# A table that gives every step of the prologue and of the first four chunks its own place, with the low half of the hidden layer issued one slot later

## The chip, the cores and the metric

One core of a Trainium2 chip runs the whole kernel. The time is device microseconds of one execution. Before the change three runs gave 982.63 us as the median (981.52 to 983.33).

## The reference

```python
def _attn_ref(q, k, v):                  # q, k, v: (8, 8, 576, 64)
    ...
    mask_plain = (rel >= 0) & (rel < window)                                     # heads 0-3, window 32
    mask_dil = (rel >= 0) & (rel < window * dilation) & (rel % dilation == 0)    # heads 4-7, dilation 4
    ...
    scores = np.where(masks[None, :, :, :], scores, -1000000000.0)
    scores = scores - np.max(scores, axis=-1, keepdims=True)
    attn = np.exp(scores)
    attn = attn / (np.sum(attn, axis=-1, keepdims=True) + 1e-09)
    return np.matmul(attn, v)

def _moe_ref(x, U, V, w_ch1, w_ch2):     # x: (8, 576, 512), U: (576, 32), V: (32, 576)
    xt = x.transpose(0, 2, 1)
    h = xt @ U @ V
    u = x + h.transpose(0, 2, 1)
    ch = np.maximum(u @ w_ch1, 0.0) @ w_ch2     # 512 -> 2048 -> 512
    return u + ch
```

A banded attention over 8 batches gives x; a mixing of rank 32 along the tokens is added to x; a two-layer network with 2048 hidden units and a ReLU follows, added to its own input. U, V, w_ch1 and w_ch2 come as 64-bit floats and are narrowed on the chip.

## The kernel before

**Tiling.** The 4608 tokens are 36 tiles of 128. The network works through them in 12 chunks: chunk 0 has four tiles, chunk 1 two, the others three. For each of 16 slices f of the hidden layer a chunk computes ph (12 matmuls, line 872) from the input and the first layer's weights, each split into a high and a low part; ACT makes hh = relu(ph) rounded (line 877), DVE makes the rest, hl = relu(ph) - hh (line 878), and the products of slice f-1 with the second layer go into acc, three matmuls per tile (line 891: hh with the high weight, hh with the low weight, hl with the high weight). So hl of slice f is wanted only after the ph of slice f+1 and the first two matmuls of acc f.

**Attention** goes in groups g of two blocks of 64 queries, nine groups to a batch (g = 0 to 71). A group's steps are: scores (PE, line 302), add (DVE, 313), top (DVE, 321), exp (ACT, 331 in the prologue, 333 later), the transposition of the weights (on PE and a copy by ACT, 339 and 345/348, for g below 18; on DVE, 355, after that), the products with v (PE, 373), and the weighting of the result (`weighted`: DVE 386, 387, 413), which also frees the PSUM bank. `burst(g, p)` puts the products of group p and the scores of group g on PE; `after_burst` is the weighting of p and the add of g.

**Mixing** of a batch b: `split_x` (ACT 446, POOL 447; 463 and 465 in the prologue) splits x into two parts, `t_mm` (PE 494; 484 and 480 in the prologue) multiplies by U, `t_evict` (501, 502) brings it to SBUF, `mix` (PE 511) multiplies by V and `mix_add` (DVE 517) adds it to x. `lay_x`, `lay_mix`, `split_sums` (PE 526 and 532, ACT 542, DVE 544) build the input of chunk 0. `turn_x` and `take_x` (DVE 563, DMA 567 and 574) transpose later tiles through DRAM.

**Weights.** The 32 pieces (j odd: the first layer's, j even: the second layer's, from j = 1 on) are fetched, then put through five stages: `w_first` (ACT 176, 177), two merges on DVE (181, 185), the high part (ACT 242), the low part (line 245: POOL, or DVE where j % 3 == 2). They are made in the course of chunk 0.

**Order.** Each engine works its queue in order, and the order is the program's. The prologue is a loop over s = 0 to 10, with lists that say what is added after which step. From chunk 0 on the network's loop calls `slot()` twice within ph, once after hl, and once after each tile of acc (7 slots to a slice in chunk 0, 5 in chunk 1, 6 later). A sorted list holds everything else with the slot at which it is issued:

```python
    def slot():
        n_slot[0] += 1
        while queue and queue[0][0] <= n_slot[0]:
            queue.pop(0)[2]()
```

`step_at(g)` is the slot of the burst of group g, between marks in STEP_AT, and every other step of g stands a number of slots behind it.

Of the kernel before, what the change touches and what calls it, by code (L numbers as in the profile page):

```python
# [123 lines left out]
def attention_moe_kernel(ctx: ExitStack, tc: tile.TileContext, qk, vv, masks, ident, ut, vt, w1, w2, out):  # L124
# [253 lines left out]
    def weighted(g):  # L378
# [26 lines left out]
        for dst, row, both in parts:  # L405
            rs = slice(row, P if both == 2 else row + QB)
            for u, pv in enumerate(pvs):
                o = dst[rs, u * P:(u + 1) * P].rearrange("p (h d) -> p h d", d=D)
# [4 lines left out]
                nc.vector.tensor_tensor(out=o, in0=pv[rs, :, 0:D],  # L413
                                        in1=ssum[rs, u].unsqueeze(2).broadcast_to([rs.stop - rs.start, 2, D]), op=ALU.mult)
# [262 lines left out]

    def both(fn, *args):
        return lambda: fn(*args)

    todo = {"act": [(2, v_steps[0]), (3, u_steps[0]), (4, both(split_v, 0)), (5, both(split_u, 0)), (6, both(keep_v, 0)), (7, both(keep_v, 1))],
            "dve": [(3, v_steps[1]), (3, v_steps[2]), (4, u_steps[1]), (4, u_steps[2])],
            "pool": [(5, both(split_v, 1)), (6, both(split_u, 1))]}
    for s, i, c in ((4, 1, 1), (5, 2, 1), (6, 3, 1), (7, 4, 1), (7, 0, 1), (8, 4, 0), (8, 0, 0), (9, 1, 0), (10, 2, 0)):
        todo["act"].append((s, both(split_first, i, c)))
        todo["pool"].append((s + (s < 10), lambda i=i, c=c: rest[i, c]()))
# [47 lines left out]
    t_first(1, 0)
    t_first(2, 0)
    t_first(3, 0)
    lay_x(2, 0)
    lay_x(CT, 0)
    for t in range(2):
        split_sums(t, 1, 1)  # L740
    t_evict(0, 0)
    for t in range(CT + 1):
        lay_mix(t, 0)
        split_sums(t, 0, 0)
    for t in range(2, CT + 1):
        split_sums(t, 1, 1)
    for t in range(CT + 1):
        split_sums(t, 0, 1)
        sums.pop(t)
    for s in range(NGB + LAG, NGB + LAG + 4):  # L750
        run_todo("act", s)
        run_todo("dve", s)
# [33 lines left out]
    LAST = [step_at(2 * NGB - 1) + 9.6, step_at(2 * NGB - 1) + 13.1]  # L786
    for i, at_ in enumerate(LAST):
        g = 2 * NGB - LAG + i
        add(step_at(2 * NGB - 1) + 1 + i, take_v, g)
        add(at_, burst, -1, g)  # L790
        add(at_ + 1, after_burst, -1, g)
    for g in range(NGB, NG + LAG):
        at_ = step_at(g)
# [23 lines left out]
    for b in range(1, B):
        for c in (1, 0):
            if c == 1:
                first = step_at(NGB * b + ODD + LAG) + (9 if b == 1 else 12)  # L820
# [157 lines left out]
```

## Time and profile before

| | |
|---|---|
| median of three runs | 982.63 us (981.52 to 983.33) |
| the profiled execution | 982.7 us, span 980.8 us |
| PE, DVE, ACT, POOL busy | 942.0, 600.0, 281.1, 109.3 us |
| instructions on PE / DVE / ACT / POOL | 9000 / 1953 / 735 / 139 |
| DMA | 94.30 MB, 96 GB/s over the span |

The span leaves 1.9 us of the profiled execution outside. A busy time of PE does not say that PE ran at its best pace: matmuls are pipelined, and one that has started late or runs slowly counts as busy. Idle time of PE with the name of what ended it, stage by stage, and the pitch from one matmul to the next are read instead.

### The profile page before, as it was taken

The page shows a single profiled execution, that of the slowest core. Times are in us where ns is not written, and L with a number is a line of the kernel's source. Part 1 is how long each engine was busy: PE and PEld are TensorE (multiplying, and loading weights), DVE is VectorE, ACT ScalarE, POOL GpSimd, SP SyncE. Part 2 cuts the span into 40 slices and gives each one's busy share as a digit, 9 for nine tenths or more (in the row PEclk, how much of TensorE's full clock was granted, in tenths as well). Part 3 has the DMA queues.
Part 4 walks back from the last instruction along what each step waited for, and adds up shares of the span by engine and source line. Part 5 has one row for each costly group of instructions (what it writes and reads, how often), then busy time and mean ns, then how long its engine had stood idle before and what let it go on. Part 6 is the DMA issues. An engine that isn't in the chain of part 4 may idle for free.

```text
span 980.8 us, 22338 instructions
## 1 busy us (share of the span) xinstructions
PE 942.0 (96%) x9000; PEld 815.3 (83%) x9000; DVE 600.0 (61%) x1953; ACT 281.1 (29%) x735; POOL 109.3 (11%) x139
## 2 busy tenths in 40 slices
PE   6999989989999999999999999999999999999998
PEld 4777668878878788888888888888888889999997
DVE  5677776877768777666766766756766753211211
ACT  4687662222212232122222222122211311111110
POOL 4332251001100110010100110010100100000000
PEclk9999999999999999999999999999999999999999
DMA  9577632243243224132233322322224201101000
GB/s 328 153 222 237 215 107 90 85 137 92 64 134 99 60 75 127 61 112 69 87 86 93 102 70 77 113 83 80 81 61 120 82 23 34 54 22 43 33 1 33
DMA packets 79144, 94.30 MB, mean 96 GB/s; under 512 B 8256, under 2 KB 57536, under 8 KB 79040
## 3 DMA queue, kind: packets, MB, share of 16 engines
q1 hardware_dynamic: 79040, 92.86, 30.5%
q8 instruction: 71, 1.16, 0.5%
q14 instruction: 33, 0.27, 0.1%
HBM read 70.81 MB, written 22.02 MB: 95 GB/s over the span
## 4 chain that ended last, share of the span: by engine, by line
PE 72%; DVE 9%; issue 9%; ACT 5%; POOL 3%; DMA 2%; SPq 1%; POOLq 0%; ACTq 0%; DVEq 0%
PE ph L872 33%; PE acc L891 31%; PE att L302 2%; POOL xhl L447 2%; DVE pt L355 2%; PE att L373 2%; ACT p L333 1%; PE t L494 1%; ACT hh L877 1%; DMA qk<-qk 1%; DVE vw L185 1%; PE m L511 1%; DMA v<-vv 1%; DVE top L321 1%; DVE p L313 1%
## 5 line engine op out<-in xcount | busy, mean ns | idle before, releaser
L878 DVE SCALAR_TENSOR_TENSOR hl<-ph,hh 128x384 fp32r<-128x384 f32 (+2 forms) x192 | 106.9, 557 | 275.4 <-ACT hh L877 274.0
L891 PE MATMUL acc<-w2h,hh 128*128 128x512 f32 x576 | 229.2, 398 | 2.8 <-ACT hh L877 2.8
L891 PE MATMUL acc<-w2h,hl 128*128 128x512 f32 x576 | 228.0, 396 | 2.0 <-DVE hl L878 2.0
L891 PE MATMUL acc<-w2l,hh 128*128 128x512 f32 x576 | 227.6, 395 | 2.3 <-POOL w2l L245 2.3
L355 DVE STREAM_TRANSPOSE pt<-p 32x64 f32<-32x64 f32 x864 | 203.8, 236 | 33.8 <-ACT p L333 20.3
L877 ACT ACTIVATE hh<-ph 128x384 fp32r<-128x384 f32 (+2 forms) x192 | 93.6, 488 | 455.3 <-PE ph L872 451.8
L872 PE MATMUL ph<-uth,w1h 128*128 128x384 f32 (+2 forms) x768 | 168.1, 340 | 0.1
L872 PE MATMUL ph<-uth,w1l 128*128 128x384 f32 (+2 forms) x768 | 167.4, 339 | 0.0
L872 PE MATMUL ph<-utl,w1h 128*128 128x384 f32 (+2 forms) x768 | 166.6, 338 | 0.0
L872 PEld LDWEIGHTS ph<-uth,w1h 128*128 128x128 f32 x768 | 135.6, 189 | 17.0 <-ACT uth L598 0.6
L872 PEld LDWEIGHTS ph<-uth,w1l 128*128 128x128 f32 x768 | 133.7, 188 | 4.0
L872 PEld LDWEIGHTS ph<-utl,w1h 128*128 128x128 f32 x768 | 132.5, 188 | 3.8
L891 PEld LDWEIGHTS acc<-w2h,hl 128*128 128x128 f32 x576 | 108.4, 188 | 27.6 <-DVE hl L878 3.7
L891 PEld LDWEIGHTS acc<-w2h,hh 128*128 128x128 f32 x576 | 108.6, 189 | 21.6 <-ACT hh L877 3.4
L891 PEld LDWEIGHTS acc<-w2l,hh 128*128 128x128 f32 x576 | 108.5, 188 | 18.7 <-POOL w2l L245 3.1
L447 POOL TENSOR_TENSOR xhl<-x,xhl 128x256 fp32r<-128x256 f32 (+1 forms) x70 | 52.5, 762 | 606.5 <-ACT xhl L446 426.9
L333 ACT ACTIVATE p<-p,top 128x64 f32<-128x64 f32 x252 | 68.9, 337 | 164.4 <-DVE top L321 164.3
L302 PE MATMUL att<-qk 64*32 64x64 f32 x2304 | 43.8, 236 | 9.4 <-DMA qk<-qk 6.2
L302 PEld LDWEIGHTS att<-qk 64*32 64x32 f32 x2304 | 34.7, 111 | 13.5 <-DMA qk<-qk 6.2
L313 DVE SCALAR_TENSOR_TENSOR p<-att,mask_sb 128x128 f32<-128x128 f32 x144 | 34.4, 279 | 13.7 <-PE att L302 13.5
L373 PEld LDWEIGHTS att<-v,pt 64*32 64x32 f32 x2016 | 19.3, 106 | 21.8 <-issue 18.0
L446 ACT CAST xhl<-x 128x256 fp32r<-128x256 f32 (+1 forms) x70 | 26.6, 401 | 27.6 <-DVE x L413 14.8
(94 smaller groups left out, 630.6 us busy)
## 6 DMA issues: line engine op xcount, KB each, us to landing
qk<-qk SPq DMA_DIRECT2D x64, 288.0 KB, 3.9
v<-vv SPq DMA_DIRECT2D x126, 130.0 KB, 3.5
raw<-w SPq DMA_DIRECT2D x25, 512.0 KB, 4.4
out<-x SPq DMA_DIRECT2D x36, 256.0 KB, 2.1
zd<-z SPq DMA_DIRECT2D x120, 64.0 KB, 1.8
xt<-zd SPq DMA_DIRECT2D x30, 256.0 KB, 2.7
xd<-xp SPq DMA_DIRECT2D x32, 128.0 KB, 2.1
x<-xd SPq DMA_DIRECT2D x32, 128.0 KB, 2.6
```

The lines of the kernel that those rows point to most:

```text
L185: nc.vector.scalar_tensor_tensor(out=vi, in0=vi, scalar=3, in1=s32, op0=ALU.logical_shift_left, op1=ALU.bitwise_or)
L302: nc.tensor.matmul(att[h][r * WIN:(r + 1) * WIN, u * KB:(u + 1) * KB], lhsT=q_, rhs=k_, start=True, stop=True, tile_position=(h * D, r * WIN))
L313: nc.vector.scalar_tensor_tensor(out=p_sb[:, h], in0=att[h][:, 0:2 * KB].rearrange("p (u k) -> p u k", k=KB), scalar=1.0 / 8.0, in1=m, op0 ...
L333: nc.scalar.activation(out=p4[:, n], in_=p4[:, n], func=AF.Exp, bias=top[:, n:n + 1])
L355: nc.vector.transpose(out=pts[g % 2][ks, :, rs], in_=p_sb[rs, :, u, WIN * k:WIN * (k + 1)])
L373: nc.tensor.matmul(att[u][row:row + WIN, o:o + DV], lhsT=pt[us_, h, WIN * r:WIN * (r + 1)], rhs=loaded[g, 1][r // 2][us_, r % 2, h * DV:(h ...
L446: nc.scalar.copy(out=xhl[rs, 0], in_=x[rs])
L447: nc.gpsimd.tensor_tensor(out=xhl[rs, 1], in0=x[rs], in1=xhl[rs, 0].bitcast(F32), op=ALU.subtract)
L872: nc.tensor.matmul(ph, lhsT=w[:, k, :], rhs=u[:, k, :], start=(n == 0 and m == 0), stop=(n == 2 and m == KC - 1))
L877: nc.scalar.activation(out=hh, in_=ph, func=AF.Relu)
L878: nc.vector.scalar_tensor_tensor(out=hl, in0=ph, scalar=0.0, in1=hh.bitcast(F32), op0=ALU.max, op1=ALU.subtract)
L891: nc.tensor.matmul(acc[i], lhsT=h[:, ss], rhs=w, start=(c > 1 and f == 1 and n == 0), stop=(f == FC and n == 2))
```

## The change

The prologue's loop is replaced by a list of named steps. Each has a place (a number) and the steps that must stand before it; the places are in the table `AT`, where a name with no entry keeps the default. The list is sorted by place and issued. From chunk 0 on, the numbers that set the queue's slots come from `AT` as well, by phase (batch 1, batch 2, batch 3, later); the weighting and the add after a burst, which were one step, have slots of their own; the slot after hh comes before hl, so that what is queued for it stands ahead of hl on DVE. The instructions themselves are the same.

```diff
-STEP_AT = [(NGB, 2), (2 * NGB - 1, 81), (2 * NGB, 114), (3 * NGB + 1, 232), (4 * NGB + 1, 342), (NG + 1, 914)]
-TURN_AT = 48
-TURN_PE = 6
-TURN_GAP = 8
+AT = {'steps': [[9, 4.732], [17, 81], [18, 109.122], [28, 232], [37, 340.452], [46, 485], [55, 628], [64, 771], [73, 914]],
+ 'lead': [[9.462, 8, 6.301, 5.806, 2.002], [9.827, 9.12, 7.708, 7, 5]],
...
+ 'hl': [1, 1, 1, 1],
...
+ 'add': [0.569, 1, 1, 1],
+ 'top': [1.5, 1.044, 1.5, 1.5],
+ 'exp': [2.684, 2, 2, 2],
+ 'exp_gap': [0.5, 0.5, 0.5, 0.5],
+ 'turn_pe': [6.353, 7],
...
+ 'scores 8': 6.609,
...
-    for s in range(NGB + LAG):
-        if s < NGB:
-            att = banks(s, "acc")
-            scores(s, att)
...
+    def do(name, at_, after, fn, *args):
+        steps.append((name, AT.get(name, at_), after, lambda: fn(*args)))
...
+        do(one("scores", g), g, [one("scores", g - 1), one("add", g - 2)], lambda g=g: scores(g, banks(g, "acc")))
+        do(one("add", g), g + 0.4, [one("scores", g), one("add", g - 1), one("turn", g - 2)], soft_add, g)
...
+            pos[name] = max([at_] + [resolve(a) + 1e-4 for a in after])
...
+    for e in sorted(steps, key=lambda e: pos[e[0]]):
+        e[3]()
...
-        for n, lead in enumerate((10, 8, 7, 5, 4)):
+        for n, lead in enumerate(AT["lead"][layer]):
...
-        add(at_ + 1, after_burst, g if g < NG else -1, p_)
+        if p_ >= 0:
+            add(at_ + AT["x"][m], evict, p_)
...
+        add(at_ + AT["add"][m] + 0.01, soft_add, g)
...
                 nc.scalar.activation(out=hh, in_=ph, func=AF.Relu)
+                if AT["hl"][min(c, 3)]:
+                    slot()
                 nc.vector.scalar_tensor_tensor(out=hl, in0=ph, scalar=0.0, in1=hh.bitcast(F32),
                                                op0=ALU.max, op1=ALU.subtract)
                 ht[f] = (hh, hl)
-                slot()
+                if not AT["hl"][min(c, 3)]:
+                    slot()
```

Some slots, worked out from the numbers of both tables (a step is issued at the first slot not below its number):

| step | slot before | slot now |
|---|---|---|
| group 15: burst, add, weighting of 13 | 62, 63 (weighting first) | 62, 63 (add first) |
| group 15: exp, transposition on PE | 64 and 65, 68 | 65 and 66, 69 |
| weighting of group 17, second merge of piece 29 | 96, 95 | 95, 96 |
| low part of piece 28 (second layer, slice 13) | 94, behind three splits more | 93 |
| high part of piece 31 (second layer, slice 15) | 107 | 105 |
| group 24: burst, weighting of 22, top, exp | 185, 186, 187, 187 and 188 | 183, 184, 184, 185 and 186 |
| tiles 9 to 11: turn_x | 257, ahead of the weighting and the add of a burst | 261, behind them |
| batch 3, first half: five mixes | 323 to 339, four slots apart | 318 to 329, about three apart |

**Prologue, PE**, from the transposition of group 6 (p_483) to the scores of group 8 (qk_137). `vps` is the second product that picks V, `t` the product with U of two parts of x. Before:

```order
L339 MATMUL ptp<-id_sb,p_483 128x128 x2
L638 MATMUL vps_555<-vhl,picks 128x176 x4
L484 MATMUL t_560<-xhl_1_1_373,ud 128x256 x2
L484 MATMUL t_560<-xhl_2_1_433,ud 128x256 x2
L302 MATMUL att_0_587<-qk_137 32x64 x4
L302 MATMUL att_1_588<-qk_137 32x64 x4
```

Now, from the end of the scores of group 7 (qk_133) to the products of group 5 (v_131):

```order
L400 MATMUL att_0_514<-qk_133 32x64 x4
L400 MATMUL att_1_515<-qk_133 32x64 x4
L400 MATMUL att_0_532<-qk_137 32x64 x4
L400 MATMUL att_1_533<-qk_137 32x64 x4
L400 MATMUL att_0_532<-qk_137 32x64 x4
L400 MATMUL att_1_533<-qk_137 32x64 x4
L471 MATMUL pv_0_553<-v_131,pt_78 32x65 x4
L471 MATMUL pv_1_554<-v_131,pt_78 32x65 x4
```

The scores of group 8 stand right behind those of group 7, ahead of the second pick product and of both products with U; the products with U now come after the transposition of group 7.

**Chunk 0, DVE, around slot 63**: hl of slice 9, the weighting of group 13 (ssum13, xp13, x8), the add (p15) and the top of group 15. Before:

```order
L878 SCALAR_TENSOR_TENSOR hl0_9_1607<-ph0_9_1549,hh0_9_1606 128x512
L386 TENSOR_SCALAR ssum13_1610<-att15_0_1564 128x2
L386 TENSOR_SCALAR ssum13_1610<-att15_1_1565 128x2
L387 RECIPROCAL ssum13_1610<-ssum13_1610 128x4
L413 TENSOR_TENSOR xp13_1614<-att15_0_1564,ssum13_1610 64x128
L413 TENSOR_TENSOR xp13_1614<-att15_1_1565,ssum13_1610 64x128
L413 TENSOR_TENSOR x8_1615<-att15_0_1564,ssum13_1610 64x128
L413 TENSOR_TENSOR x8_1615<-att15_1_1565,ssum13_1610 64x128
L313 SCALAR_TENSOR_TENSOR p15_1621<-att15_0_1564,mask_sb_71 128x128
L313 SCALAR_TENSOR_TENSOR p15_1621<-att15_1_1565,mask_sb_71 128x128
L321 TENSOR_REDUCE top15_1624<-p15_1621 128x4
```

Now:

```order
L411 SCALAR_TENSOR_TENSOR p15_1610<-att15_0_1568,mask_sb_71 128x128
L411 SCALAR_TENSOR_TENSOR p15_1610<-att15_1_1569,mask_sb_71 128x128
L484 TENSOR_SCALAR ssum13_1613<-att15_0_1568 128x2
L484 TENSOR_SCALAR ssum13_1613<-att15_1_1569 128x2
L485 RECIPROCAL ssum13_1613<-ssum13_1613 128x4
L507 TENSOR_TENSOR xp13_1617<-att15_0_1568,ssum13_1613 64x128
L507 TENSOR_TENSOR xp13_1617<-att15_1_1569,ssum13_1613 64x128
L507 TENSOR_TENSOR x8_1618<-att15_0_1568,ssum13_1613 64x128
L507 TENSOR_TENSOR x8_1618<-att15_1_1569,ssum13_1613 64x128
L969 SCALAR_TENSOR_TENSOR hl0_9_1607<-ph0_9_1545,hh0_9_1606 128x512
L419 TENSOR_REDUCE top15_1629<-p15_1610 128x4
```

The add went ahead of the weighting, and hl from ahead of both to behind both.

**End of chunk 0, POOL**: the splits of batch 1 (xhl1_i_c) and the low parts of pieces 27 and 28 (w1l, w2l). Before:

```order
L447 TENSOR_TENSOR xhl1_3_1_1990<-x7_1644,xhl1_3_1_1990 128x256
L245 TENSOR_TENSOR w1l_13_1893<-vw27_1924,w1h_13_1892 128x4x128
L447 TENSOR_TENSOR xhl1_4_1_2016<-x8_1615,xhl1_4_1_2016 128x256
L445 MEMSET xhl1_0_0_2043 64x512
L447 TENSOR_TENSOR xhl1_0_0_2043<-x4_496,xhl1_0_0_2043 64x256
L447 TENSOR_TENSOR xhl1_1_0_2047<-x5_1640,xhl1_1_0_2047 128x256
L245 TENSOR_TENSOR w2l_13_1895<-vw28_1956,w2h_13_1894 128x512
```

Now:

```order
L542 TENSOR_TENSOR xhl1_3_1_2021<-x7_1644,xhl1_3_1_2021 128x256
L343 TENSOR_TENSOR w1l_13_1893<-vw27_1927,w1h_13_1892 128x4x128
L343 TENSOR_TENSOR w2l_13_1895<-vw28_1955,w2h_13_1894 128x512
L542 TENSOR_TENSOR xhl1_4_1_2041<-x8_1618,xhl1_4_1_2041 128x256
L540 MEMSET xhl1_0_0_2067 64x512
L542 TENSOR_TENSOR xhl1_0_0_2067<-x4_498,xhl1_0_0_2067 64x256
```

The low part of piece 28 went ahead of four entries of the splits, three of which work on x and one of which clears a tile.

More of the change, by code (lines that the diff above doesn't have):

```diff
@@ L71 @@
 SCRATCH = 1024
-STEP_AT = [(NGB, 2), (2 * NGB - 1, 81), (2 * NGB, 114), (3 * NGB + 1, 232), (4 * NGB + 1, 342), (NG + 1, 914)]
-TAIL_1, TAIL = 1.4, 2.2
-TURN_AT = 48
-TURN_PE = 6
-TURN_GAP = 8
+AT = {'steps': [[9, 4.732], [17, 81], [18, 109.122], [28, 232], [37, 340.452], [46, 485], [55, 628], [64, 771], [73, 914]],
+ 'lead': [[9.462, 8, 6.301, 5.806, 2.002], [9.827, 9.12, 7.708, 7, 5]],
+ 'fetch': [23.034, 12],
+ 'hl': [1, 1, 1, 1],
+ 'last': [9.913, 13.1],
+ 'x': [0.836, 0.864, 1, 1],
+ 'add': [0.569, 1, 1, 1],
[3 more added lines that the diff above has]
+ 'turn_pe': [6.353, 7],
+ 'turn': [0, 0.392, 0.454, 0.35],
+ 'turn_gap': [0, 0.107, 0.1, 0.1],
+ 'cast1': [-2.727, 1.248, 3.543, 0.293, 1.5, 0.57],
+ 't1': [2.426, 0.3, 6.516, 0.219],
+ 'mix1': [4, 2.468, 16, 1.546],
+ 'cast': [[0, 0], [12, 1.747], [12, 1.8], [12, 1.8]],
+ 'cast_gap': [0, 1.131, 1, 1],
+ 't': [0.3, 5, 5, 5],
+ 'mix': [0.1, 4, 4, 4],
+ 'mix_gap': [[0, 0], [3, 4], [2.687, 4], [3, 4]],
+ 'mix_add': [1, 0.743, 0.607, 1],
+ 'flip': [36.156, 6.472, 4],
+ 'x 3': 5.346,
+ 'mix (2, 0)': 12.211,
+ 'v 1': 3.963,
+ 'sub 2': 1.006,
+ 'low 6': 9.479,
+ 'fetch 1': 3.411,
+ 'hi (0, 0)': 11.474,
+ 'top 6': 6.383,
+ 'w0 2': 8.995,
+ 'exp 0': -1.015,
+ 'lo (3, 0)': 12.003,
+ 'hi (1, 0)': 11.213,
+ 'lo (1, 1)': 12.027,
+ 'v 2': 2.601,
+ 'fetch 4': 8.08,
+ 'w1 3': 11.591,
+ 'lo (0, 0)': 12.074,
+ 'scores 8': 6.609,
+ 'fetch 5': 12.824,
+ 'scores 1': 1.044,
+ 'add 2': 2.433,
+ 'keep_v 1': 8.225,
+ 'lo (0, 1)': 12.219,
+ 'mix (0, 0)': 11.711,
+ 'top 8': 8.461,
+ 'w1 1': 11.006,
+ 'u 0': 4.034,
+ 'cast 3': 7.149,
+ 'pv 8': 10.274,
+ 'u 1': 5.708,
+ 'x 7': 9.32,
+ 'hi (1, 1)': 10.906,
+ 'scores 6': 5.854,
+ 't 1': 7.85,
+ 'low 8': 10.877,
+ 'hi (0, 1)': 10.873,
+ 'mix (1, 0)': 11.832,
+ 't 9': 11.537,
+ 'exp 6': 6.897,
+ 'mix (3, 1)': 10.15,
+ 'pv 7': 9.26,
+ 'low 2': 7.813,
+ 'lay (3, 0)': 12.297,
+ 'top 2': 2.544,
+ 'exp 1': 2.277,
+ 'pick_v 0': 6.29,
+ 'split_u 0': 4.154,
+ 'hi (3, 0)': 14.256,
+ 'cast 2': 4.432,
+ 'turn 5': 6.487,
+ 'turn 8': 8.221,
+ 'split_v 1': 4.688,
+ 'lay (2, 1)': 11.553,
+ 'low 5': 10.117,
+ 'add 0': -0.052,
+ 'add 5': 5.11,
+ 'lay (1, 0)': 9.896,
+ 'qk 1': 10.986,
+ 'copy 8': 9.514,
+ 'copy 1': 2.142,
+ 'low 1': 6.43,
+ 'x 1': 3.635,
+ 'copy 0': 0.616,
+ 'lo (2, 1)': 11.823,
+ 'sub 0': -0.377,
+ 'scores 7': 6.688,
+ 'fetch 6': 11.596,
+ 'hi (2, 0)': 12.12,
+ 'fetch 3': 12.575,
+ 'add 8': 7.826,
+ 'cast 5': 9.371,
+ 'x 0': 2.778,
+ 'copy 4': 4.781,
+ 'cast 4': 8.393,
+ 'ts 1': 9.38,
+ 't 6': 10.93}
@@ L678, in both @@
[L678 to L686, printed above, removed]
@@ L734, in attention_moe_kernel @@
[L734 to L741, printed above, removed]
-    for t in range(CT + 1):
[L743 to L752, printed above, removed]
+    steps = []
@@ L753, in attention_moe_kernel, with resolve @@
+    pos = {}
+    known = {e[0]: e for e in steps}
+    def resolve(name):
+        if name in known and name not in pos:
+            _, at_, after, _ = known[name]
+            pos[name] = max([at_] + [resolve(a) + 1e-4 for a in after])
+        return pos.get(name, -1.0)
+    for e in steps:
+        resolve(e[0])
+    for e in sorted(steps, key=lambda e: pos[e[0]]):
+        e[3]()
+    sums.clear()
     early_open.close()
@@ L815, in attention_moe_kernel @@
     mixed_at = {}
     for b in range(1, B):
+        m = phase(b)
+        parts_ = batch_parts(b)
+        n = len(parts_)
         for c in (1, 0):
[L819 to L824 removed]
```

222 lines of the change are left out of this document (112 added, 110 removed).

## The prediction

> **What bounds the kernel now.** I read the busy times first, then the same by stage, then what PE waited for in each stage, then the instructions around the longest waits. The stages are the prologue, chunks 0 to 3 one by one, chunks 4 to 10, and the last chunk.
>
> ```profile
> span 980.8 us, 22338 instructions
> PE 942.0 (96%) x9000; PEld 815.3 (83%) x9000; DVE 600.0 (61%) x1953; ACT 281.1 (29%) x735; POOL 109.3 (11%) x139
> ...
> 0.00:41.40 41.40, 30.58 (x670) 24.32 (x670) 23.09 (x86) 20.36 (x50) 19.72 (x34) 1.00 0.78 262
> 41.40:160.30 118.90, 109.82 (x1037) 85.32 (x1036) 86.61 (x188) 82.06 (x192) 38.97 (x33) 1.00 0.54 170
> 160.30:219.50 59.20, 55.06 (x685) 47.33 (x684) 47.28 (x176) 14.22 (x47) 0.00 (x0) 0.98 0.42 127
> 219.50:303.00 83.50, 80.48 (x879) 69.62 (x877) 60.96 (x226) 21.16 (x63) 8.75 (x13) 1.00 0.29 87
> 303.00:385.00 82.00, 78.86 (x816) 68.38 (x815) 61.19 (x221) 20.79 (x59) 7.65 (x11) 1.00 0.29 88
> 385.00:910.00 525.00, 520.24 (x4586) 460.02 (x4586) 309.14 (x1040) 114.68 (x309) 34.20 (x48) 1.00 0.25 75
> ```
>
> PE is the bound, so the change can only win where PE stands still or runs slowly. Its idle time by stage (length less PE busy) is 10.8 us in the prologue, 9.1 in chunk 0, 4.1 in chunk 1, 3.0 in chunk 2, 3.1 in chunk 3 and 4.8 in the 525 us after that. The granted clock of 0.98 in chunk 1 adds 2% of 59.2, 1.2 us, at a lower pace. What the change reaches with effect is thus some 20 us in chunks 0 to 3 and a part of the prologue. What PE waited for, in the order of those stages:
>
> ```profile
> PE att L302 <- DMA qk<-qk: 6.2, 4, 3.7
> ...
> PE att L339 <- ACT p L333: 3.7, 6, 1.3
> PE acc L891 <- POOL w2l L245: 2.3, 2, 1.4
> PE att L373 <- issue: 1.4, 1, 1.4
> PE t L494 <- DVE x L413: 1.2, 1, 1.2
> ...
> PE acc L891 <- ACT hh L877: 2.8, 2, 2.1
> PE att L373 <- DMA v<-vv: 1.1, 2, 0.7
> ...
> PE acc L891 <- DVE hl L878: 1.7, 1, 1.7
> ...
> PE m L511 <- DVE x L517: 3.0, 4, 1.6
> ```
>
> The first row is the prologue's: groups wait for their q and k, the loads stand in the same order before and after, and I leave it untouched. The other rows are chunk 0 (four), chunk 1 (two), chunk 2 and chunk 3. Each is a step that stood late in the queue of DVE, ACT or POOL, engines that are 80% busy at most (DVE in chunk 1, 47.28 of 59.2).
>
> **The prologue: -1.** The chain of waits passes nearly all of it through PE:
>
> ```profile
> 21.74 0.79 PE vps L638 x4
> ...
> 24.53 0.06 issue
> ...
> 26.14 1.24 PE t L484 x4
> 27.39 0.61 PE att L302 x32
> ...
> 32.60 2.56 PE tp L526 x12
> 35.16 0.62 PE pv L373 x32
> ...
> 39.62 0.98 PE tp L526 x8
> ...
> 41.48 1.51 PE L872 MATMUL ph<-uth,w1h 128*128 128x512 f32 x4
> ```
>
> The only long detour is from 24.53 to 26.14: PE's queue has a product with U at its head that waits for two other engines, and the scores of group 8 stand behind it until 27.39. The change takes these scores ahead of it. Of the 1.6 us, 0.8 are the second pick product (a first one takes 0.79 in the chain), work that PE must do anyway, so 0.8 us is what can go. One `lay_x` moves from behind the products of group 8 to ahead of them. It is four instructions, at 2.56/12 = 0.213 us each ahead of 35 us and 0.98/8 = 0.122 behind it: it costs 0.85 there and saves 0.5, which gives back 0.4. The last `split_sums` stand closer behind their matmuls, which I take as 0.5. Together about -1; bounds +0.5 (group 8's exp, now wanted earlier by PE, arrives late) and -2.5 (the whole detour and a bubble at the end).
>
> [...]
>
> **Chunk 0, transpositions on PE: -3.** The largest of the six waits of 3.7 us in total:
>
> ```profile
> 103.30 0.69 DVE L878 SCALAR_TENSOR_TENSOR hl<-ph,hh 128x512 fp32r<-128x512 f32 x1 [1.31 <-ACT hh L877]
> ...
> 105.39 0.49 DVE L313 SCALAR_TENSOR_TENSOR p<-att,mask_sb 128x128 f32<-128x128 f32 x2
> ...
> 106.37 0.59 ACT L333 ACTIVATE p<-p,top 128x64 f32<-128x64 f32 x2 [3.11 <-DVE top L321]
> ...
> 108.04 0.56 ACT L333 ACTIVATE p<-p,top 128x64 f32<-128x64 f32 x2
> ...
> 108.66 0.33 PE L339 MATMUL att<-id_sb,p 128*128 128x128 f32 x1 [1.32 <-ACT p L333]
> ```
>
> DVE stood idle 1.31 us for hh, did hl (0.69), then the weighting of group 13 (from hl's end at 103.99 to 105.39, 1.4 us), then the add. Now the add comes first of these and hl last. From 101.99 on, where DVE was free, add, weighting and hl take 0.49 + 1.4 + 0.69, so the top behind them starts at about 104.6 instead of 105.9. The two halves of exp are no longer parted by a first stage of a weight piece (106.96 to 108.04 on ACT), so the second half ends some 2 us earlier, and the transposition stands a slot later, about 0.85 us (118.9 us over some 112 slots and a few dozen bursts and products). That is more than the 1.32. The other waits are shorter and have the same two cures. I take 3.0 of 3.7; bounds 0 and -3.7.
>
> **End of chunk 0: -3.5.**
>
> ```profile
> 138.61 1.01 DVE L413 TENSOR_TENSOR x<-att,ssum 64x128 f32<-64x128 f32 x4
> ...
> 142.21 1.27 POOL L245 TENSOR_TENSOR w2l<-vw,w2h 128x512 fp32r<-128x512 f32 x1
> ...
> 155.57 0.63 ACT L242 CAST w2h<-vw 128x512 fp32r<-128x512 f32 x1
> ...
> 156.27 1.30 POOL L245 TENSOR_TENSOR w2l<-vw,w2h 128x512 fp32r<-128x512 f32 x1 [7.03 <-ACT w2h L242]
> ```
>
> The second row is piece 28, late behind splits: it goes ahead of four of their entries, so the 1.4 us go. The fourth is piece 31, late because its high part (third row) stood behind the eviction of two tiles; its slot is two earlier, which is more than the 0.9 that remain of the 2.3. The wait of 1.2 is for the weighting of group 17 (first row), which held a bank; it now goes ahead of the second merge of piece 29: 0.9 of it. The 1.4 put down to "issue" fits the same kind of wait one group earlier (group 16's weighting); its place hardly changes, and I count 0.4. Sum 2.3 + 0.9 + 0.4 = 3.6, taken as 3.5; bounds -1 and -5.
>
> **Chunk 1: -3.5.**
>
> ```profile
> 214.94 0.42 DVE L321 TENSOR_REDUCE top<-p 128x4 f32<-128x256 f32 x1
> 215.40 1.06 ACT L333 ACTIVATE p<-p,top 128x64 f32<-128x64 f32 x4 [5.42 <-DVE top L321]
> 216.37 0.36 ACT L877 ACTIVATE hh<-ph 128x256 fp32r<-128x256 f32 x1
> ...
> 216.78 0.79 PE L891 MATMUL acc<-w2h,hh 128*128 128x512 f32 x1 [2.08 <-ACT hh L877]
> ```
>
> ACT had nothing to do for 5.42 us, but exp of group 24 stood ahead of the last hh, and waited for a top that DVE did late. Burst, add and top now stand two to three slots earlier (a slot here is 59.2/80 = 0.74 us): 1.5 to 2.2 us, about the 2.08. The slow stretch begins right behind this wait, and I count 0.9 of its 1.2 us with it. Of the other 0.7 for hh and the 1.1 for v (the loads stood behind the transposed tiles on SP's queue, whose turn is now earlier) I count 0.5. Sum 3.5; bounds +1 (DVE is 80% busy and the wait comes elsewhere) and -5.5.
>
> **Chunks 2 and 3: -2.5.** The 1.7 for hl is DVE held up by the third of three `turn_x`, which waits for the store of the first:
>
> ```profile
> 280.67 0.71 DVE L563 STREAM_TRANSPOSE z<-x 128x512 f32<-128x512 f32 x1 [3.38 <-DMA zd<-z]
> ```
>
> They stay three in one slot, but behind the burst's weighting, add and top instead of ahead, in the slots after one hl and well ahead of the next; I count 1.5. Of the 3.0 for `mix_add` the five mixes of batch 3's first half lie where two bursts met them; they now fall almost between two bursts, though three slots apart instead of four: 1.0. Bounds +1 and -4.5.
>
> **New waits: +2.** hl moves behind what is queued for its slot. That cost is not in the trace, since hl made only the one wait. The cover is about one slice, 59.2/16 = 3.7 us in chunk 1, and what may stand ahead is a weighting, an add and a top (1.4 + 0.49 + 0.42 above, 2.3 us), with hl's own 0.69 then 3.0. So 0.7 us of cover is left at worst, and a DVE with a backlog eats it. The low parts that DVE makes for the first layer stand two slots ahead of their slice instead of four, some 1.7 us less of cover, in five pieces. I take +2 for all; bounds 0 and +4 short of the rival below. After 385 us nothing but hl, tile turns and the order within a burst changes, over 4.8 us of idle: 0, bounds -1 and +1.
>
> **Sum.** -1 - 3 - 3.5 - 3.5 - 2.5 + 2 = -11.5, against the profiled execution of 982.7 us (span 980.8, 1.9 around it): 971.2. The median is 0.1 below the profiled execution and asks for no correction. I round towards no change, 972.
>
> **Rivals.**
>
> 1. The waits move rather than go. DVE in chunk 1 (80%) and ACT in chunk 0 (82.06 of 118.9) have the same work to do; what goes ahead pushes something else back. For it: the same steps appear in several waits. Against it: ACT stood idle for 5.42 and 3.11 us just ahead of the two longest ones. Half the sum: 977.
> [...]
> 3. Slower: hl late at each burst. In chunks 0 to 3 there are some 27 bursts after the first few groups; if DVE's backlog at hl exceeds the 0.7 us of cover by 0.5 on the mean of all of them, PE loses 27 x 0.5 = 13.5 us and the sum becomes +2: 985. It decides from a mean loss of 0.45 us per burst on. For it: DVE's share of 80%. Against it: DVE waits 274.0 us for hh over the span, and that wait is just where hl stood,
>
> ```profile
> DVE hl L878 <- ACT hh L877: 274.0, 151, 4.3
> ```
>
> so that work put ahead of hl fills idle time first.
> 4. The change doesn't do what it says: a step runs when its inputs are there, whatever its place, since DVE and ACT have idle time in every stage. 982. Against it: each queue runs in order, and the waits quoted are those of a ready step behind one that isn't.
>
> **How the numbers follow.** Forecast (968 to 975.5) 0.48; rival 2 and other better cases (below 968) 0.13; rival 1 (975.5 to 980.5) 0.20; rival 4, within 0.2% of 982.6, 0.09; rival 3, slower, 0.10. 0.2% is about what a measurement of this kernel can tell from no change. Faster 0.81, same 0.09, slower 0.10. The range, 964 to 982, leaves out the best few per cent, most of rival 3 and part of rival 4.
>
> **What would show it.** Right: ph of chunk 0 starts near 40.5 us instead of 41.48; no wait of line 339's transpositions over 0.5 us; no wait of acc for w2l; the end of chunk 1 without a wait for hh and with a granted clock of 1.00; waits for hl under 2 us in all. Wrong: waits of acc for hl in chunks 0 and 1 at every burst, w1l waits on PE in chunk 0, a slow stretch of PE elsewhere, or a DVE share near 90% in chunk 1.

## The result, and the profile after

The changed kernel takes 957.25 us (median of four runs, three of them at 955.9 to 957.25) against 982.54 us: a ratio of 0.9739, 95% interval [0.9719, 0.9758]. On another chip it took 955.27 us, ratio 0.9725 [0.9711, 0.9740]. The gain is 25 to 27 us; 10.7 were forecast, and 957 lies below the range. One of the first four runs, the profiled one, had a granted clock of 0.66 and took 1305.5 us, so the trace shown is that of the second chip (span 953.5 us, 955.3 us in all).

The page of after: busy times, then the stages with the columns that the prediction showed (length, PE, PEld, DVE, ACT, POOL, granted clock, DMA share, GB/s). The stages begin at the first ph of chunks 0 to 4 and of chunk 11:

```profile
span 953.5 us, 22326 instructions
PE 930.9 (98%) x9000; PEld 811.2 (85%) x9000; DVE 603.0 (63%) x1953; ACT 283.2 (30%) x735; POOL 111.0 (12%) x139
...
0.00:39.49 39.49, 27.23 (x671) 21.38 (x671) 24.40 (x88) 21.24 (x52) 21.71 (x35) 0.96 0.83 274
39.49:153.19 113.70, 110.06 (x1068) 85.48 (x1068) 88.68 (x189) 81.44 (x189) 37.80 (x33) 1.00 0.58 182
153.19:206.16 52.97, 52.41 (x654) 46.31 (x653) 47.06 (x176) 14.88 (x48) 0.23 (x1) 1.00 0.44 133
206.16:284.92 78.76, 78.66 (x879) 69.28 (x878) 61.65 (x226) 20.72 (x62) 9.02 (x13) 1.00 0.31 92
284.92:364.33 79.41, 78.01 (x815) 68.55 (x813) 60.21 (x219) 21.10 (x59) 7.71 (x11) 1.00 0.32 93
364.33:882.58 518.25, 517.40 (x4584) 459.72 (x4585) 309.16 (x1041) 115.99 (x309) 34.51 (x48) 1.00 0.26 76
```

Chunk 0 is 5 us shorter than before, chunk 1 is 6, chunks 2 and 3 together 7, and chunks 4 to 10 another 6.6, though PE's idle time in them had been only 4.8. The busy time of PE fell too, 942.0 to 930.9 us for the same 9000 matmuls. What PE waited for in after (total, times, longest):

```profile
PE att L400 <- DMA qk<-qk: 7.9, 5, 3.6
...
PE ph L961 <- ACT uth L694: 1.7, 2, 1.3
...
PE ph L961 <- DVE w1l L343: 1.0, 2, 0.7
PE att L437 <- ACT p L431: 0.8, 1, 0.8
...
PE acc L983 <- DVE hl L969: 0.4, 1, 0.4
```

The waits for w2l, hh and mix_add's x are gone, that for exp (p) is 0.8 instead of 3.7, and the later hl makes PE wait 0.4 us in all. New are waits for w1l, 1.0 us in chunk 0, which the prediction had named as a sign of being wrong. DVE's own wait at hl, 274.0 us in 151 cases before, is still there, but shorter:

```profile
DVE hl L969 <- ACT hh L966: 231.6, 133, 3.9
```

The table shows the lengths of the stages in us for all 18 kernels run and for before, read from the first ph of each chunk in the timeline (what lies behind chunk 10 is 67.1 us of PE work in each). The time is the median, the ratio that to before on the same chip.

| kernel | time | ratio [95%] | prologue | c0 | c1 | c2+c3 | c4 to c10 |
|---|---|---|---|---|---|---|---|
| before | 982.5 | 1 | 41.5 | 118.8 | 59.2 | 165.5 | 524.9 |
| after_again | 955.3 | 0.9725 [0.9711, 0.9740] | 39.5 | 113.7 | 53.0 | 158.2 | 518.3 |
| hl_alone | 966.4 | 0.9824 [0.9806, 0.9843] | 40.0 | 114.2 | 57.5 | 161.4 | 520.8 |
| hl_back | 976.4 | 0.9932 [0.9915, 0.9949] | 40.6 | 121.8 | 54.4 | 162.6 | 524.6 |
| queue_back | 964.1 | 0.9814 [0.9790, 0.9838] | 41.1 | 113.1 | 55.9 | 161.3 | 520.9 |
| queue_back_first | 956.7 | 0.9732 [0.9717, 0.9746] | 40.8 | 113.7 | 52.9 | 158.6 | 518.4 |
| queue_back_later | 960.9 | 0.9776 [0.9762, 0.9791] | 41.3 | 113.7 | 53.3 | 160.1 | 520.7 |
| prologue_back | 956.4 | 0.9736 [0.9722, 0.9751] | 40.2 | 115.1 | 52.2 | 157.9 | 518.0 |
| hl_chunk0 | 966.8 | 0.9831 [0.9810, 0.9850] | 41.3 | 113.7 | 54.1 | 161.9 | 523.5 |
| hl_ahead_of_other | 973.4 | 0.9912 [0.9894, 0.9929] | 41.1 | 122.1 | 53.3 | 161.7 | 522.9 |
| hl_ahead_of_soft | 961.6 | 0.9788 [0.9773, 0.9802] | 40.4 | 116.7 | 54.6 | 159.0 | 518.3 |
| weights_behind | 965.6 | 0.9820 [0.9794, 0.9845] | 40.6 | 122.1 | 53.0 | 158.1 | 518.1 |
| turns_behind | 964.7 | 0.9808 [0.9787, 0.9828] | 40.0 | 113.8 | 53.3 | 161.5 | 521.9 |
| no_hl_after | 951.6 | 0.9687 [0.9673, 0.9701] | 41.6 | 111.7 | 52.0 | 157.1 | 516.1 |
| no_hl_before | 958.4 | 0.9753 [0.9738, 0.9767] | 39.6 | 113.5 | 54.1 | 157.7 | 518.9 |
| hl_two_slots | 958.4 | 0.9742 [0.9720, 0.9764] | 39.6 | 112.7 | 53.4 | 159.9 | 519.5 |
| hl_two_chunk0 | 955.2 | 0.9719 [0.9703, 0.9734] | 41.0 | 112.6 | 52.9 | 157.8 | 518.3 |
| first_back_w2 | 960.4 | 0.9780 [0.9766, 0.9793] | 41.7 | 117.2 | 52.4 | 157.5 | 518.3 |
| first_back_w2_hl2 | 960.4 | 0.9782 [0.9769, 0.9795] | 41.3 | 116.6 | 52.7 | 157.7 | 518.5 |

### The profile page after: what moved, and what is told of

The parts are those of the page before. It is cut to its first block, busy times and chain, and to the rows that moved or that the text cites. A ratio compares the mean times of both kernels' runs of the same rounds, so it can differ in the third digit from the quotient of the medians.

```text
span 1303.8 us, 22326 instructions
## 1 busy us (share of the span) xinstructions
PE 1288.4 (99%) x9000; PEld 938.4 (72%) x9000; DVE 605.8 (46%) x1953; ACT 283.3 (22%) x735; POOL 109.4 (8%) x139
## 4 chain that ended last, share of the span: by engine, by line
PE 98%; DMA 1%; issue 0%; SPq 0%; DVE 0%; ACT 0%
PE ph L961 44%; PE acc L983 44%; PE att L400 2%; PE att L471 2%; PE t L590 2%; PE m L607 1%; DMA qk<-qk 1%; PE tp L622 0%; PE pv L471 0%; PE t L580 0%; PE ptp L437 0%; PE att L437 0%; PE tp L684 0%; PE acc L652 0%; PE tp L628 0%
## 5 line engine op out<-in xcount | busy, mean ns | idle before, releaser
L983 PE MATMUL acc<-w2h,hh 128*128 128x512 f32 x576 | 296.7, 515 | 0.0
L983 PE MATMUL acc<-w2h,hl 128*128 128x512 f32 x576 | 295.6, 513 | 0.0
L983 PE MATMUL acc<-w2l,hh 128*128 128x512 f32 x576 | 295.4, 513 | 0.0
L961 PE MATMUL ph<-uth,w1h 128*128 128x384 f32 (+2 forms) x768 | 227.3, 432 | 0.0
L961 PE MATMUL ph<-uth,w1l 128*128 128x384 f32 (+2 forms) x768 | 226.9, 430 | 0.0
L961 PE MATMUL ph<-utl,w1h 128*128 128x384 f32 (+2 forms) x768 | 226.3, 429 | 0.0
L961 PEld LDWEIGHTS ph<-uth,w1h 128*128 128x128 f32 x768 | 156.8, 211 | 56.7 <-issue 16.8
L961 PEld LDWEIGHTS ph<-utl,w1h 128*128 128x128 f32 x768 | 155.3, 210 | 33.2 <-issue 4.7
L961 PEld LDWEIGHTS ph<-uth,w1l 128*128 128x128 f32 x768 | 153.9, 211 | 33.7 <-issue 5.0
L613 DVE TENSOR_TENSOR x<-x,m 128x256 f32<-128x256 f32 (+1 forms) x66 | 27.7, 419 | 45.4 <-PE m L607 30.5
```

Of the source, the lines that this page charges most:

```text
L613: nc.vector.tensor_tensor(out=x, in0=x, in1=mixed.pop((b, i, c))[rs], op=ALU.add)
L961: nc.tensor.matmul(ph, lhsT=w[:, k, :], rhs=u[:, k, :], start=(n == 0 and m == 0), stop=(n == 2 and m == KC - 1))
L983: nc.tensor.matmul(acc[i], lhsT=h[:, ss], rhs=w, start=(c > 1 and f == 1 and n == 0), stop=(f == FC and n == 2))
```

## The experiments

**Three parts, put back one at a time.** The change has a prologue, a set of numbers for the queue, and hl's place. Each of three kernels puts one back, by the table `AT` alone:

```diff
--- hl_back
- 'hl': [1, 1, 1, 1],
+ 'hl': [0, 0, 0, 0],
--- queue_back: every number from 'steps' to 'flip' but 'hl', so
+ 'steps': [[9, 2], [17, 81], [18, 114], [28, 232], [37, 342], [73, 914]],
+ 'lead': [[10, 8, 7, 5, 4], [10, 8, 7, 5, 4]],
...
--- prologue_back: the named places
- 'x 3': 5.346,
- 'mix (2, 0)': 12.211,
...
```

after_again: 

> The changed kernel once more, for an undisturbed profile: 957 us (955 to 959). Theory A (the order of the queue's steps in chunks 0 to 3 took the gain): the first four chunks are together over 18 us shorter than before and the chunks behind them at most 3 us shorter. Theory B (the later place of hl took the 14 us that the forecast lacks): every chunk is 1 to 2 us shorter, the last eight together over 8 us. Theory C (the prologue): the first ph of chunk 0 starts at or before 30 us instead of 41.48.

hl_back: 

> hl goes back to its place ahead of the slot; prologue and queue numbers are the new ones. Theory A: 955 to 958, hl's place costs or gives at most 2 us. Theory B: about 971, since 14 of the 25 us hang on hl. Theory C: 957.

queue_back: 

> The numbers of the queue (all steps from chunk 0 on) go back to those of before; the new prologue and the later hl stay. Theory A: 975 to 982, most of the gain is lost. Theory B: 966 to 970 (12 us lost, the share that the forecast gave to the queue). Theory C: 966 to 970 likewise.

prologue_back: 

> The named places of the prologue's steps are left out, so that their defaults give the order of before; the queue's numbers and the later hl stay. Theories A and B: 958 to 959 (the forecast's 1 us). Theory C: about 971.

Measured 955.3, 976.4, 964.1 and 956.4. Putting hl back costs 21 us, the queue's numbers 8.8; the prologue's 1.1 is hardly clear of the noise (the ratios are 0.9736 and 0.9725). The first four chunks are 18.7 us shorter, as theory A had it, but hl_back, at 976 and not 955 to 958, rules A out. Theory B holds in kind and underestimates hl. Its guess that the last eight chunks shrink by over 8 us is too high (6.6 in seven of them, 0 in the last), and every theory's time for queue_back and prologue_back was some 2 us too high or more.

**hl's place alone.** All numbers and the prologue as before; the one edit to the order of before is

```diff
                 nc.scalar.activation(out=hh, in_=ph, func=AF.Relu)
+                slot()
                 nc.vector.scalar_tensor_tensor(out=hl, in0=ph, scalar=0.0, in1=hh.bitcast(F32), ...)
                 ht[f] = (hh, hl)
-                slot()
```

> The order and all numbers of before; the one edit is that the slot comes ahead of hl. Additive parts: 965 (queue's numbers back gave 964.1, the prologue 1.1). The forecast's reading (hl behind queue items is a cost of 0 to 4 us): 983 to 987.

Measured 966.4, 17.1 us less than the 983.5 of before on that chip: nearly two thirds of the whole gain from one line, and within 1.4 us of the 965 of additive parts. How it comes is seen at the longest wait for mix_add, at 342 us. The timeline of before, DVE and then PE; a row is start, us, instructions, and in brackets the idle time ahead of it:

```profile
340.26 0.56 DVE L878 SCALAR_TENSOR_TENSOR hl<-ph,hh 128x384 fp32r<-128x384 f32 x1 [1.30 <-ACT hh L877]
340.83 0.49 DVE L355 STREAM_TRANSPOSE pt<-p 32x64 f32<-32x64 f32 x2
...
341.83 1.01 DVE L413 TENSOR_TENSOR x<-att,ssum 64x128 f32<-64x128 f32 x4
342.77 0.47 DVE L313 SCALAR_TENSOR_TENSOR p<-att,mask_sb 128x128 f32<-128x128 f32 x2
343.27 0.42 DVE L321 TENSOR_REDUCE top<-p 128x4 f32<-128x256 f32 x1
343.61 0.41 DVE L517 TENSOR_TENSOR x<-x,m 128x256 f32<-128x256 f32 x1
...
344.07 0.38 PE L511 MATMUL m<-ts,vs 128*128 128x256 f32 x1 [1.57 <-DVE x L517]
```

DVE stood 1.30 us at hl; two transpositions, a weighting, an add, a top and a mix_add were queued behind it, and the last of them held a bank that PE needed, for 1.57 us. The same place in hl_alone:

```profile
328.80 1.25 DVE L377 STREAM_TRANSPOSE pt<-p 32x64 f32<-32x64 f32 x5
...
330.56 1.01 DVE L431 TENSOR_TENSOR x<-att,ssum 64x128 f32<-64x128 f32 x4
331.49 0.47 DVE L335 SCALAR_TENSOR_TENSOR p<-att,mask_sb 128x128 f32<-128x128 f32 x2
331.89 0.54 DVE L893 SCALAR_TENSOR_TENSOR hl<-ph,hh 128x384 fp32r<-128x384 f32 x1
332.35 0.40 DVE L343 TENSOR_REDUCE top<-p 128x4 f32<-128x256 f32 x1
332.68 0.40 DVE L537 TENSOR_TENSOR x<-x,m 128x256 f32<-128x256 f32 x1
...
333.14 0.39 PE L531 MATMUL m<-ts,vs 128*128 128x256 f32 x1
```

Transpositions, weighting and add fill the time up to hl, hl has nothing to wait for, and m starts without a wait. In the first of the two pieces DVE idled 1.30 us with two transpositions next in line, whose input had been there since ACT's last exp ended at 334.18 us: none of what stood behind hl started ahead of it.

**Without hl.** If the stand at hl is the cost, taking the instruction away must show it from both ends.

```diff
-                nc.vector.scalar_tensor_tensor(out=hl, in0=ph, ...)
-                ht[f] = (hh, hl)
+                ht[f] = (hh, hh)
```

no_hl_after: 

> The new kernel without the computation of hl: the third product of a slice reads hh in place of hl, so PE's work is the same and DVE has 192 instructions fewer. Theory F (what cost time was that DVE's queue stood at hl until hh was there): 949 to 955, little is left to gain. Rival G (DVE's load, of which hl is some 0.65 us x 192 = 125 us, still slows the new kernel): under 945.

no_hl_before: 

> The order and the numbers of before in all places, with hl left out in the same way. Theory F: 958 to 964, the whole worth of hl's move (18 us) comes from taking the instruction away. Rival H (the order of the other steps counts, not the stand at hl): over 970.

Measured 951.6 and 958.4. The order of before loses 24 us with its hl, the new kernel only 3.7: theory F, and G and H are out. Of the 24, 17 come back by moving hl alone. So the 231.6 us that DVE still stands at hl in after cost at most these 3.7: what matters is not how long DVE stands but whether PE waits for something queued behind hl.

**Which steps hl held up.** In the new kernel the steps of hl's slot are sorted: some stay ahead of hl, some go behind it.

```diff
+    behind = W_STAGES + [turn_dve, mix_add, t_evict, turn_x, take_x]                     # hl_ahead_of_other
+    behind = [evict, soft_add, soft_top, soft_exp, split_x, take_rows]                   # hl_ahead_of_soft
+    behind = W_STAGES                                                                    # weights_behind
+    behind = [turn_dve, mix_add, t_evict, turn_x, take_x]                                # turns_behind
...
-                if AT["hl"][min(c, 3)]:
-                    slot()
+                kept = slot_split()        # issues the slot's steps, gives back those in behind
                 nc.vector.scalar_tensor_tensor(out=hl, in0=ph, ...)
+                for e in kept:
+                    e[2]()
```

hl_ahead_of_other: 

> The new kernel, but of the steps in hl's slot only the weighting, add and top stay ahead of hl on DVE; the merges and low parts of weights, turn_dve, turn_x, t_evict and mix_add go behind it. Theory D (what hl held up was the softmax chain, add, top and weighting, for which PE waits through exp): 956 to 961, nearly all of the gain stays. Theory E (what it held up was the making of weights, the transpositions on DVE and mix_add): 968 to 977, near the 976.4 of hl back in its place.

hl_ahead_of_soft: 

> The mirror image: in hl's slot the weighting, add, top (and exp and the splits that need them) go behind hl, the weights' stages, transpositions and mix_add stay ahead of it. Theory D: 968 to 977. Theory E: 956 to 961.

weights_behind: 

> The new kernel; of the steps in hl's slot only the stages of the weight pieces (merges and low parts) go behind hl. They exist in chunk 0 alone. Theory E1 (they are what hl held up in chunk 0): 962 to 965, with chunk 0 near 121.5 us instead of 113.7 and the rest as in the new kernel. Rival E2 (the 8 us of chunk 0 come from several kinds of steps together): 956 to 961.

turns_behind: 

> The mirror image: turn_dve, mix_add, t_evict, turn_x and take_x go behind hl in hl's slot, the weights' stages stay ahead. Theory E1: 962 to 965, with chunk 0 unchanged (113 to 115 us), chunks 3 and 4 some 2.4 us longer each. Rival E2: near 970, as when both kinds go behind (973.4).

Measured 973.4 and 961.6: theory E in the main, 0.6 us over its range in the second. With only the softmax steps ahead of hl 3 of the 21 us remain; with only the others ahead, 15, so the softmax steps matter too, by some 6. weights_behind and turns_behind give 965.6 and 964.7 (E1 had 962 to 965 for both), and by stages E1 holds. With the weights' stages behind hl, chunk 0 is 122.1 us and every other stage that of the new kernel; with the transpositions and mixing behind it, chunk 0 is 113.8 and the later ones are longer by 3.3 (chunks 2 and 3) and 3.7 us (4 to 10). What PE waits for in chunk 0 of weights_behind:

```profile
PE att L472 <- ACT pt L447: 3.2, 5, 0.8
PE ph L975 <- DVE w1l L344: 3.2, 2, 1.8
PE att L438 <- ACT p L432: 2.6, 4, 1.4
PE att L472 <- issue: 1.3, 1, 1.3
```

The weights themselves are 3.2 of it. The rest are softmax steps, probably pushed back on DVE and ACT by merges that come later. In chunk 0 of hl_back the same four waits stand at 3.1, 3.2, 2.3 and 1.3 us. All this holds for the new numbers; which steps hl held up under the old ones was not sorted out in this way. In turns_behind from chunk 1 on the first row is a mix_add again:

```profile
PE m L608 <- DVE x L614: 3.0, 6, 0.7
```

**hl by chunks, and later still.** hl_chunk0 has `'hl': [1, 0, 0, 0]`. hl_two_slots issues hl behind the slot of the first tile of acc, hl_two_chunk0 does that in chunk 0 alone:

```diff
                     slot()
+                    if i == 0 and f < FC:
+                        low_half(*ht[f])        # the instruction that makes hl
```

hl_chunk0: 

> The new kernel with hl late in chunk 0 alone and back in its place from chunk 1 on. If the two effects are apart (weights' stages in chunk 0, transpositions and mixing later): chunk 0 is 113 to 115 us, the later chunks as with hl back, 965 to 970. If a late chunk 0 is what delays the later ones: 956 to 960.

hl_two_slots: 

> The new kernel with hl one slot later still, behind the slot of the first tile of acc. Theory F (hl's stand cost time and is now nearly gone: without hl at all it is 951.6): 953 to 957, within the 3.7 us that are left. Rival 3 of the forecast (an hl that comes late holds PE at acc): 960 to 975, with waits of acc for hl of over 5 us in all.

hl_two_chunk0: 

> The new kernel with hl two slots behind hh in chunk 0 and one slot behind it later. By the chunk times of the run with two slots everywhere (112.7 us for chunk 0 against 113.7, later chunks longer): 953.5 to 955.5, up to 1.5 us under the new kernel. If DVE's order in chunk 0 no longer matters: 955 to 957.

hl_chunk0 gives 966.8, chunk 0 as in the new kernel and the later ones nearly as in hl_back: the two effects are separate. hl_two_slots gives 958.4, 1.4 us over the range that theory F gave. DVE's wait at hl falls again, and PE begins to wait for hl:

```profile
DVE hl L949 <- ACT hh L970: 180.8, 97, 3.9
...
PE acc L984 <- DVE hl L949: 3.2, 7, 0.7
```

This is rival 3's mechanism, a slot further on and with a small price. hl_two_chunk0 takes 1.1 us from chunk 0 in the trace, and 955.2 us is the same as 955.3. On the chip of these two runs the second slot from chunk 1 on costs 3.2 us, with ranges of single runs that just touch (956.45 to 959.61 and 954.75 to 956.68). So one slot is about the best place.

**The queue's numbers by phase.** With hl late, the numbers of the first phase (groups 9 to 17, batch 1, weights) or of the later ones go back:

```diff
--- queue_back_first
+ 'steps': [[9, 2], [17, 81], [18, 109.122], ...], 'lead': [[10, 8, 7, 5, 4], [10, 8, 7, 5, 4]],
+ 'x': [0.98, ...], 'add': [0.99, ...], 'exp': [1.99, ...], 'turn_pe': [6, 7], 'cast1': [-4, 1.2, 2.5, 0.6, 1.5, 0.5], ...
--- queue_back_later
+ 'steps': [..., [28, 232], [37, 342], [73, 914]], 'cast_gap': [0, 2, 2, 2], 'mix_gap': [[0, 0], [4, 3], ...],
+ 'flip': [48, 8, 4], ...
--- first_back_w2: queue_back_first, and
- 'lead': [[10, 8, 7, 5, 4], [10, 8, 7, 5, 4]],
+ 'lead': [[10, 8, 7, 5, 4], [9.827, 9.12, 7.708, 7, 5]],
--- first_back_w2_hl2: first_back_w2 with hl two slots behind hh in chunk 0
```

queue_back_first: 

> The new kernel with only the numbers of the first phase (groups 9 to 17, batch 1, the weights' stages and fetches) back to those of before, hl late. Theory Q (with hl late the numbers of chunk 0 are worth little, since the same waits are gone by hl's move alone): 955 to 958. The forecast's terms (3 + 3.5 of 12.5 us in chunk 0): 960 to 962.

queue_back_later: 

> The new kernel with only the numbers of the later phases (groups from 18 on, batches 2 to 7, tile turns) back, hl late. Theory Q: 961 to 964, nearly all of the 8.8 us, in chunks 1, 2 and 4 to 10. The forecast's terms (3.5 + 2.5 us in chunks 1 to 3, 0 behind them): 959 to 961.

first_back_w2: 

> The new kernel with the first phase's numbers of before, except that the stages of the second layer's pieces keep their new places. With the first phase's numbers back, chunk 0 was as long as in the new kernel (113.7 us) with 2.3 us of it in waits for w2l and no wait at the transpositions on PE. If the new places for these pieces take those waits away by themselves: chunk 0 is 111 to 112.5 us and the time 953 to 955. If they bring the transpositions' waits back: 955 to 957.5.

first_back_w2_hl2: 

> The same with hl two slots behind hh in chunk 0. If the waits that hl's second slot freed in the new kernel's chunk 0 (1.1 us) are those that the old numbers had not: as the kernel beside it, within 1 us. If they add: 952 to 954.

The later phases are worth 5.6 us (960.9). By the time alone that fits the forecast's terms, and is 0.1 under theory Q's range; the stages speak for Q, since 2.4 of it lie in chunks 4 to 10, where the forecast had nothing. The first phase is worth 1.5 at most (956.7; the new kernel itself took 955.3 on one chip and 957.2 on another), and none of that lies in chunk 0, which is 113.7 us with either set. Yet the waits of chunk 0 in queue_back_first are those that the prediction had named:

```profile
PE acc L984 <- POOL w2l L344: 2.3, 2, 1.4
PE t L591 <- DVE x L508: 1.3, 1, 1.3
PE att L472 <- issue: 1.0, 1, 1.0
```

There is none at the transpositions on PE, though. With the second layer's stages at their new places (first_back_w2) the wait for w2l goes, and

```profile
PE att L438 <- ACT p L432: 3.0, 4, 1.1
PE t L591 <- DVE x L508: 1.9, 1, 1.9
PE att L472 <- ACT pt L447: 1.0, 1, 1.0
```

come instead: 960.4, chunk 0 117.2. The better of the two guesses was 953 to 955, and the worse one was too good as well. With hl two slots behind hh in chunk 0 (first_back_w2_hl2) it is 960.4 again. No kernel with the same computation beats the new one by more than the measurement can tell.

## Why the prediction was wrong in size

The sign was right. Against the spans (980.8 and 953.5), term by term:

| term | forecast | measured | hl_alone |
|---|---|---|---|
| prologue | -1 | -2.0 in these two traces | -1.5 |
| chunk 0 (transpositions -3, its end -3.5) | -6.5 | -5.1 | -4.6 |
| chunk 1 | -3.5 | -6.2 | -1.7 |
| chunks 2 and 3 | -2.5 | -7.3 | -4.1 |
| new waits | +2 | no loss in any stage; waits of 0.4 for hl and 1.0 for w1l | waits of 3.0 for hl (2.0 before) |
| after 385 us | 0 | -6.6 | -4.0 |

**The step that failed is "New waits: +2", bounds 0 and +4.** Outside the one place that the transpositions' term looks at, it priced hl's move only by what a later hl could hold up, and excluded a gain. The move is the largest part of the change, some 17 us alone and 21 in the new kernel. The row with 274.0 us of DVE standing at hl was in the prediction, and beside rival 3 it said that work put ahead of hl fills idle time first. That was used against a loss; what this work, standing behind hl until then, had cost PE was not asked. Of the 24 us that no_hl_before shows, little could be read from the names of PE's waits: they name exp and mix_add, not the hl ahead of these on DVE. The waits for w2l are another matter: 2.2 of their 2.3 us stay both in hl_alone and in no_hl_before, so they are not hl's.

**After 385 us: 0.** In the main the same step. The prediction let only hl, the tile turns and the order within a burst change there, "over 4.8 us of idle"; but 4.3 of this idle time stand before the products with U, and hl had a part in them. These products wait for splits of x on POOL and ACT, and ACT's splits wait in turn for the weighting on DVE (13.8 us in six waits, before), or stand behind an exp that waits for a top on DVE (88.6 us in 29). In chunks 4 to 10, before, then hl_alone, then after:

```profile
L494 PE MATMUL t<-xhl,us 128*128 128x256 f32 x80 | 17.2, 298 | 4.3 <-POOL xhl L447 2.8 <-ACT xhl L446 1.1 <-POOL xhl L445 0.2
```

```profile
L514 PE MATMUL t<-xhl,us 128*128 128x256 f32 x80 | 15.6, 288 | 1.8 <-POOL xhl L466 1.2 <-ACT xhl L465 0.5
```

```profile
L590 PE MATMUL t<-xhl,us 128*128 128x256 f32 x80 | 14.9, 282 | 0.0
```

From before to after they lose 4.3 us of idle time and 2.3 of busy time, as much as the whole 6.6. hl_alone has 4.0 of that. The other 2.5 are the numbers of the later phases (queue_back_later, 520.7 against 518.3, has the 1.8 us of hl_alone again; with hl left out of the order of before 1.6 stay). For these the premise was wrong: from batch 3 on one half of the splits now stand one slot apart instead of two, and the two spacings of the mixes change places. Which of these numbers does it was not tested.

**Chunks 2 and 3: -2.5.** The waits named were the right ones, and they went. But the mix_add waits were put down to the spacing of the mixes. The mixing products of these two chunks in before, in hl_alone, which has the old spacing, and in after:

```profile
L511 PE MATMUL m<-ts,vs 128*128 128x256 f32 x20 | 6.1, 305 | 3.5 <-DVE x L517 3.5
```

```profile
L531 PE MATMUL m<-ts,vs 128*128 128x256 f32 x20 | 5.9, 294 | 0.5 <-DVE x L537 0.4
```

```profile
L607 PE MATMUL m<-ts,vs 128*128 128x256 f32 x20 | 5.7, 285 | 0.0
```

hl's move took 3.0 of the 3.5 us. The wait for hl behind turn_x is not among what it took: 1.3 us of the 1.7 stay in hl_alone and go with the new numbers. The gain of 7.3 is more than all idle time of these chunks (6.1): PE's busy time in them fell too, by 2.7.

**Chunk 1: -3.5.** The wait for hh is gone and the granted clock is 1.00, as forecast. The size was too small; the term counted only what burst, add and top gain by their slots. In hl_alone the chunk still has 57.5 us at a granted clock of 0.97. The new numbers without hl's move bring it to 54.4 (hl_back), and so does leaving hl out of the order of before (54.1, clock 1.00), so either way goes most of the distance. With only one phase's numbers put back it stays at 52.9 and 53.3; which of the numbers counts here is open. The chunk in hl_alone:

```profile
154.17:211.72 57.55, 55.27 (x686) 47.60 (x684) 46.63 (x175) 14.48 (x47) 0.00 (x0) 0.97 0.41 128
```

A group's scores, 32 matmuls and 0.6 us (320 take 5.6 in chunk 0), stand in chunk 0 now and count there.

**Chunk 0.** The transpositions' wait fell from 3.7 to 0.8, and in hl_alone it is gone with no other edit, so the -3 was right in its place and came from hl. "End of chunk 0: -3.5" was right in the waits and wrong in what they are worth: they went, and chunk 0 is as long with them (queue_back_first) as without. In part that is rival 1, the waits that move: in after w1l (1.0 us), exp (0.8) and the copies of its transpositions (0.5) have come in their place, and in first_back_w2, where only the second layer's stages go ahead, exp has 3.0. But PE's idle time in chunk 0 is still 1.4 us less in after than in queue_back_first (3.6 against 5.1), and its busy time 1.5 more (110.1 against 108.6, for the same matmuls); why is open.

**The prologue: -1** can't be seen in a trace: the first ph comes between 39.5 and 41.7 us in the 15 traces with the new order and between 39.6 and 41.5 in the four with the old. prologue_back timed 1.1 us longer, but its trace has that in chunk 0 (115.1) rather than ahead of it. PE's waits for q and k differ by more than the term from trace to trace, 6.2 to 8.7 us with the old order and 6.2 to 9.1 with the new. One thing does come with the new order. The transpositions of `lay_x`, before and then after:

```profile
32.40 2.76 PE L526 MATMUL tp<-id_sb,x 128*128 128x128 f32 x12
```

```profile
31.09 1.95 PE L622 MATMUL tp<-id_sb,x 128*128 128x128 f32 x16
```

Sixteen of them take 1.95 us, 0.122 each, in all 15 traces of the new order. Twelve took 2.42 to 2.76 in three of the four traces of the old one, and 1.50 in no_hl_before. That is the quicker of the two paces that the prediction read off, 0.122 us against 0.213, and yet no earlier first ph stands out of the spread. The clock rows don't show this pace: the granted clock is 1.00 in all of the prologue of before. No run shows what sets the pace. The forecast's 0.13 for times below 968 (rival 2 and others) counted in part on such a pace; what the runs show below 968 is hl's move, which alone reaches 966.4.

## What to carry to other kernels

When an engine stands long at one instruction, ask first what is queued behind it and who waits for that; idle time on an engine that is not the bottleneck can be the root of small waits elsewhere that bear other names, as DVE's 274.0 us at hl were here. An instruction whose result is wanted late goes behind the ready work of its engine, by about one step: here 17 us from one line, and a second step gave some 3 back. The price of a reordering is bounded from both sides until a run with the suspected instruction taken away has said what it costs.

## What was not expected of the hardware

With the waits ahead of two kinds of products, their busy time fell too. The products with U took 298 ns each on the mean with their waits and 282 without, the mixing products of chunks 2 and 3 had 305 and 285, and of the 27 us that the span lost 11 were busy time of PE with unchanged matmuls (942.0 to 930.9). Not all of that stands where waits went: some 3 lie in the prologue, where the transpositions of `lay_x` alone went from 5.9 us to 4.5, and 2.7 in chunk 1, where the granted clock went from 0.98 to 1.00 and a group's scores left; 5.4 lie in chunks 2 to 10. So PE's busy share did not tell how much was left to gain: it stood at 96% before, and 2.8% of the span went, with the busy time lower by 1.2%.
